# A fused attention and gated-MLP kernel: half-row turns and projections in the first head, two scalings on GpSimd, a half-row filler at the end

## The chip, the cores and the metric

The kernel runs on one core of a Trainium2 chip. The metric is device time in microseconds, the median of several executions. The core has TensorE (PE in the profile; its weight loads are the row PEld), VectorE (DVE), ScalarE (ACT), GpSimd (POOL), and DMA queues issued from several of them (SP issues most). Each engine works through its own list of instructions in order and waits on semaphores that other engines raise.

## The reference, cut to what matters

```python
x = A_x                                   # (1, 2048, 640), bf16
xn = _layernorm(x)                        # per row, eps 1e-5
q = (xn @ wq)                             # 32 heads of 192
p = softmax(q @ k_cache^T * 192 ** -0.5)  # 2048 keys per head
s = (p @ v_cache) @ wo                    # (6144 -> 640)
h = silu(xn @ w1) * (xn @ w3)             # 640 -> 1536
g = silu(h @ w2)                          # 1536 -> 640
return x + s * g
```

All matrices are bf16. The keys and values are inputs; only the queries are projected.

## The kernel before, in words

**Tiles.** The 2048 query rows are 16 tiles of 128 (`ln_*` functions take a tile number) or 4 chunks of 512 (`qb`). The 2048 keys of a head are taken in 8 pairs `p` of 2 x 128. `(qb, p)` below is chunk and pair of a head. The normalised rows are kept transposed in `xnT` (640 columns as 5 blocks `c` of 128 partitions, 2048 rows), and `xnS` is the same with the two 64-partition halves exchanged, copied by DMA (`swap_rows`, L344).

**One pair.** `scores` (L445) does three steps of two matmuls that use 64 rows of the array each (row halves `ROWS`), into a PSUM buffer of the pool `ps_st` (tag `st2`, two buffers). `weights` (L451) is the exponential on ScalarE, with a bias `nb` that bounds the scores so that no running maximum is needed. `values` (L491) multiplies with the values, again on two row halves, into the banks `ob0` and `ob1`; `evict` takes these to SBUF on VectorE at the end of a chunk. `advance` strings this together and leaves three or four groups of value matmuls undone, so that TensorE has work while ScalarE makes the next exponential. It also runs `extra`, work put between a pair's scores and the next pair's.

**The bound `nb`.** It needs the largest absolute query and key entries: `maxima` or a reduction on VectorE, `bound`, and an all-reduce over the partitions on GpSimd (L402). In the first head every chunk has its own `nb` (`next_bound`), later heads have one (`finish_head`). A reduction called `warm` (L539) is put early in the first head.

**The first head.** Rows are normalised while the first head already runs. `ln_stats` (VectorE) or `ln_sum` and `ln_squares` (ScalarE, for the tiles in `ASUM`) give mean and variance, `ln_root` the inverse deviation (ScalarE), `ln_scale` (L251) the scaled row `xn`. Then it is transposed: tiles 0 to 7 on TensorE (`ln_turn`, L259, copied out at L260), tiles 8 to 15 by a transposing DMA from SP's queue (`ln_send`, L271). The first head's projection (`project_chunk`, branch `h == 0`, L318) uses all 128 rows of the array; that of later heads (L323) uses `xnT` and `xnS` on two row halves. Both fill one `st2` buffer with qA (128 columns) and qF; copies give qS (qA with halves exchanged, GpSimd, L329) and qD (half of qF, GpSimd, L333). The third scoring step reads qD and qF.

**Order.** Every instruction given to `pin` keeps the order in which the program text issues it on its engine. The order in the first head is written out by hand: `posts` (after a pair), `extra_at` (inside it), `behind_at` and `key_at` (reductions for the second head). The second head's keys and values are loaded (`load_keys`) after `(1, 3)`, `(1, 5)` and `(1, 6)` of the first.

**The end.** In the last head `hidden_last` (L661) computes one block of hidden units on two row halves, for each chunk, from `xnT` and `xnS`. When the last pair's scores are done, TensorE fills the wait for the last exponentials with `ffn_hidden(0, 1)` (L636, 128 rows). Then the rest of the hidden units, `ffn_out` (L795) and `output_tile` (L774) follow. The weights `w2_sb` (L751) are loaded into memory that `xnS` leaves free.

## Time and profile before

| what | value |
|---|---|
| median of 3 executions | 1941.55 us (1941.48 to 1941.87) |
| the profiled execution | 1941.69 us, its span 1939.8 us |
| TensorE busy | 1931.3 us, VectorE 1097.1, ScalarE 1213.7, GpSimd 464.8 |
| opening, 0 to 16.5 us | TensorE busy 13.70 us |
| chunk 0 of the first head, 16.5 to 29.3 | 12.48 of 12.80 |
| chunk 1, 29.3 to 44.4 | 15.05 of 15.10 |
| chunk 2, 44.4 to 59.5 | 15.04 of 15.10 |
| chunk 3, 59.5 to 75.8 | 16.30 of 16.30 |
| heads 2 to 32, 75.8 to 1634 | 1558.20 of 1558.20 |
| end of the last head, 1634 to 1650 | 15.95 of 16.00 |
| MLP, 1650 to 1726 | 75.82 of 76.00 |
| output, 1726 to 1939.8 | 208.75 of 213.80 |

How to read it: the span runs from the first to the last instruction of the profiled execution. Rows in order of time give start, duration, engine, line, operation, output and inputs, count, and in brackets the idle time of that engine ahead of it with what ended it; rows of the same kind that lie close are merged into one, from the first start to the last modelled end. Matmuls are pipelined and their ends modelled, so distances between starts tell more than durations. Two matmuls on different row halves run at the same time. `POOLq` marks the instructions of GpSimd's sequencer, which don't count as busy.

### The profile page before, as it was taken

To read this page: it belongs to the slowest core of one execution; us is meant where nothing else is said; L and a number is where in the kernel's file an instruction comes from. 1 tells how busy PE (TensorE), PEld (TensorE's weight loads), DVE (VectorE), ACT (ScalarE), POOL (GpSimd) and SP (SyncE) were. 2 spreads that over 40 slices of the span, in tenths; PEclk is the share of its full clock that TensorE was granted. 3 is DMA by queue.
4 is the path that set the end of the run, shared out by engine and by line. 5 is a ranking of instruction groups with operands and counts; after the bars stand their busy time and mean duration, and the time that the engine had idled before them with its cause. 6 is when DMAs were issued, how large, how long until landed. Compare 5 with 4: busy or idle time off the path is not lost.

```text
span 1939.8 us, 60573 instructions
## 1 busy us (share of the span) xinstructions
PE 1931.3 (100%) x27228; PEld 1317.1 (68%) x27237; DVE 1097.1 (57%) x2267; ACT 1213.7 (63%) x1180; POOL 464.8 (24%) x769
## 2 busy tenths in 40 slices
PE   9999999999999999999999999999999999999998
PEld 5666666666666666666666666666666776577776
DVE  8765656565656565666665666656665655521111
ACT  7777777777767677777777777777777777210000
POOL 3432222222222222233222222222222210000000
PEclk9999999999999999999999999999999999999999
DMA  7621212121212222232222222212121103937882
GB/s 173 130 71 42 79 42 79 41 66 40 61 42 64 53 54 63 58 73 68 63 50 71 49 71 50 71 41 79 41 79 41 39 10 116 278 73 135 152 154 55
DMA packets 325098, 146.44 MB, mean 75 GB/s; under 512 B 275984, under 2 KB 317936, under 8 KB 324832
## 3 DMA queue, kind: packets, MB, share of 16 engines
q1 hardware_dynamic: 311184, 110.90, 24.3%
q0 software_dynamic: 8832, 26.55, 5.6%
q10 hardware_dynamic: 4816, 5.05, 1.0%
q8 instruction: 215, 3.52, 0.8%
q14 instruction: 51, 0.42, 0.1%
HBM read 56.23 MB, written 31.98 MB: 45 GB/s over the span
## 4 chain that ended last, share of the span: by engine, by line
PE 99%; ACT 0%; DVE 0%; issue 0%; POOL 0%
PE obank L491 35%; PE st L445 34%; PE ps L323 14%; PE ps_s L774 11%; PE ps_f L795 3%; PE ps_gu L636 1%; PE ps L661 0%; PE ps L318 0%; PE fill L204 0%; ACT xnT L260 0%; ACT pT L451 0%; PE pst L259 0%; POOL qS L329 0%; ACT qA L325 0%; DVE ones_w L166 0%
## 5 line engine op out<-in xcount | busy, mean ns | idle before, releaser
L451 ACT ACTIVATE pT<-st,nb 128x1024 bf16<-128x1024 f32 x1016 | 1130.4, 1113 | 438.7 <-PE st L445 437.3
L491 PEld LDWEIGHTS <-pT 64*128 64x128 bf16 x16384 | 713.2, 94 | 242.3 <-ACT pT L451 0.6
L491 PE MATMUL obank<-vt,pT 64*128 64x193 bf16 x16384 | 851.8, 243 | 0.1
L461 DVE COPY osum<-obank 128x386 f32<-128x386 f32 x256 | 142.3, 556 | 550.1 <-PE obank L491 550.1
L445 PE MATMUL st<-qS,KM 64*128 64x512 bf16 x1024 | 385.1, 376 | 0.5 <-POOL qS L329 0.3
L445 PE MATMUL st<-qA,KM 64*128 64x512 bf16 x1024 | 385.1, 376 | 0.0
L445 PE MATMUL st<-qA,KT 64*128 64x512 bf16 x1024 | 385.0, 376 | 0.0
L445 PE MATMUL st<-qS,KT 64*128 64x512 bf16 x1024 | 385.0, 376 | 0.0
L445 PE MATMUL st<-qF,KT 64*128 64x512 bf16 x1024 | 385.0, 376 | 0.0
L445 PE MATMUL st<-qD,KT 64*128 64x512 bf16 x1024 | 385.0, 376 | 0.0
L329 POOL COPY qS<-qA 64x512 bf16<-64x512 bf16 x256 | 188.7, 737 | 520.9 <-DVE qA L325 495.6
L445 PEld LDWEIGHTS <-KT 64*128 64x128 bf16 x4096 | 201.5, 94 | 135.5 <-issue 0.4
L323 PE MATMUL ps<-xnT,wq 64*128 64x512 bf16 x1240 | 288.1, 376 | 0.0
L323 PE MATMUL ps<-xnS,wq 64*128 64x512 bf16 x1240 | 286.9, 376 | 0.0
L774 PE MATMUL ps_s<-wo_sb,oT 128*128 128x320 bf16 (+2 forms) x1535 | 208.8, 299 | 0.1
L323 PEld LDWEIGHTS <-wq 64*128 64x128 bf16 x2480 | 120.4, 94 | 116.3
L774 PEld LDWEIGHTS <-oT 128*128 128x128 bf16 x1536 | 148.4, 98 | 60.4
L468 DVE TENSOR_TENSOR ostage<-osum,rl_all 128x384 bf16<-128x384 f32 x256 | 153.0, 598 | 9.0 <-DVE rl_all L467 0.3
L462 DVE TENSOR_TENSOR osum<-osum,obank 128x386 f32<-128x386 f32 x256 | 142.6, 557 | 8.9
L348 DVE TENSOR_REDUCE st<-KT 128x1 f32<-128x512 bf16 (+1 forms) x189 | 122.0, 685 | 1.2
L779 DVE SCALAR_TENSOR_TENSOR tmp<-ps_s,g_all 128x320 f32<-128x320 f32 (+2 forms) x32 | 15.6, 487 | 176.0 <-PE ps_s L774 176.0
L445 PEld LDWEIGHTS <-KM 64*128 64x128 bf16 x2048 | 100.5, 94 | 17.5 <-issue 2.3
(112 smaller groups left out, 1139.9 us busy)
## 6 DMA issues: line engine op xcount, KB each, us to landing
o_scr<-ostage SPq DMA_DIRECT2D x64, 384.0 KB, 2.8
vt<-in_A_v_cache_dram SPq DMA_DIRECT2D x62, 384.0 KB, 4.9
wo_sb<-in_A_wo_dram POOLq DMA_DIRECT2D x1, 7680.0 KB, 31.3
wq<-in_A_wq_dram POOLq DMA_DIRECT2D x31, 160.0 KB, 3.1
hT_scr<-hblk SPq DMA_DIRECT2D x16, 256.0 KB, 2.9
xnS<-xnT POOLq DMA_DIRECT2D x8, 320.0 KB, 8.0
xt<-in_A_x_dram POOLq DMA_DIRECT2D x16, 160.0 KB, 9.1
wq<-in_B_w_dram POOLq DMA_DIRECT2D x31, 80.0 KB, 2.6
```

The costliest lines, as they stand in the source:

```text
L323: pin(nc.tensor.matmul(halves[t], lhsT=wq[ROWS[t], s, :], rhs=xs[ROWS[t], s // 2, qs], start=(s == 0), stop=(s == 2 * DC - 1)))
L329: keep(nc.gpsimd.tensor_copy(out=qS[ROWS[t], qs], in_=qA[ROWS[1 - t], qs]))
L348: pin(nc.vector.tensor_reduce(out=heads[h]["st"][:, j, k:k + 1], in_=heads[h]["L"]["KT"][:, j, c0:c1], axis=AX.X, op=ALU.max, apply_absolu ...
L445: pin(nc.tensor.matmul(st2[:, t * 512:(t + 1) * 512], lhsT=k, rhs=q[ROWS[t], qs], start=(s == 0), stop=(s == 2)))
L451: pin(nc.scalar.activation(out=pT2[:], in_=st2[:], func=ACT.Exp, scale=SCALE, bias=nb[:]))
L461: pin(nc.vector.tensor_copy(out=osum[:], in_=ov[:, 0, :, 0:DH + 1]))
L462: pin(nc.vector.tensor_tensor(out=osum[:], in0=osum[:], in1=ov[:, 1, :, 0:DH + 1], op=ALU.add))
L468: pin(nc.vector.tensor_tensor(out=ostage[:, b * 2:b * 2 + 2, hg * DH:(hg + 1) * DH], in0=osum[:, :, 0:DH], in1=rl.unsqueeze(2).to_broadcas ...
L491: pin(nc.tensor.matmul(acc["o"][b][:, r, (j % 2) * 256:(j % 2) * 256 + DH + 1], lhsT=pT2[ROWS[r], t * 512 + j * P:t * 512 + (j + 1) * P], ...
L636: pin(nc.tensor.matmul(ps[:, o:o + 512], lhsT=w_sb[:, c, (fl - 1) * P:fl * P], rhs=xnT[:, c, qs], start=(c == 0), stop=(c == DC - 1)))
L774: pin(nc.tensor.matmul(ps, lhsT=oT[:, k, :], rhs=wo_sb[:, k, c0:c1], start=(k == 0), stop=(k == OC - 1)))
L795: pin(nc.tensor.matmul(ps[:, pi * 512:pi * 512 + c1 - c0], lhsT=lhs[fc], rhs=w2_sb[:, fc, c0:c1], start=(fc == 0), stop=(fc == FC - 1)))
```

## The change: what it does

- `ASUM` loses tile 15: its statistics come from VectorE (`ln_stats`), not from ScalarE.
- `ln_scale` takes an engine; tiles 8 to 11 are scaled on GpSimd, two at a time, after `(0, 5)` and `(0, 7)`. Tiles 12 to 15 stay on VectorE.
- `next_turn` (tiles 4 to 7) transposes each 128-column block as two 64-row halves, each with the identity's half, and both copies are made on VectorE.
- `first_project(0, qb)` for chunks 1 to 3 becomes `half_project(qb, 0)` and `(qb, 1)`, in two successive pairs. Each contracts the two row halves separately into the two halves of an `st2` buffer; ScalarE copies one half to SBUF (`part`), VectorE adds the other.
- The second head's key and value loads come two pairs, and one pair, later.
- `hidden_last` for the last chunk takes the place of `ffn_hidden(0, 1)` in the drain, and `ffn_hidden(0, 1)` goes to the loop behind.

```diff
@@ -177,7 +177,7 @@
             pin(nc.vector.tensor_tensor(out=ident_bf[b, b], in0=cols[b, :], in1=rows[b, :], op=ALU.is_equal))
         nsub = 2
         mv = lnx.tile([P, NQT, nc.vector.BN_AGGR_DIM], F32, name="mv")
-        ASUM = {1: 0, NQT - 1: 1}
+        ASUM = {1: 0}
         sums = lnx.tile([P, len(ASUM)], F32, name="sums")
         sqs = lnx.tile([P, len(ASUM)], F32, name="sqs")
         nmean = lnx.tile([P, len(ASUM)], F32, name="nmean")
@@ -243,12 +243,12 @@
 
         scaled = {}
 
-        def ln_scale(i0):
+        def ln_scale(i0, eng=nc.vector):
             scaled[i0] = []
             for i in range(i0, i0 + 2):
                 xn = xnp.tile([P, D], BF16, tag="xn", name="xn")
                 act = i in ASUM
-                pin(nc.vector.tensor_scalar(out=xn[:], in0=x_all[:, i, :], scalar1=a_col(nmean, i) if act else mv[:, i, 0:1],
+                pin(eng.tensor_scalar(out=xn[:], in0=x_all[:, i, :], scalar1=a_col(nmean, i) if act else mv[:, i, 0:1],
                                             scalar2=rstd[i], op0=ALU.add if act else ALU.subtract, op1=ALU.mult))
                 scaled[i0].append(xn)
 
@@ -262,11 +262,20 @@
                     for t, cp in enumerate(copies)]
 
         def next_turn(i0):
-            for copy in ln_turn(i0, (nc.scalar.copy, nc.vector.tensor_copy)):
-                copy()
-
-        def ln_send(i0):
-            ln_scale(i0)
+            pst = ps_st.tile([P, 2, 1024], BF16, tag="st2", name="pst")
+            for t, xn in enumerate(scaled.pop(i0)):
+                for c in range(DC):
+                    for r in range(2):
+                        c0 = (2 * c + t) * DT
+                        pin(nc.tensor.transpose(out=pst[:, r, c0:c0 + DT], in_=xn[ROWS[r], c * P:(c + 1) * P],
+                                                identity=ident_bf[ROWS[r], ROWS[r]]))
+            for r in range(2):
+                pin(nc.vector.tensor_copy(
+                    out=xnT[:, :, i0 * P:(i0 + 2) * P].rearrange("p c (t r q) -> p c t r q", t=2, r=2)[:, :, :, r, :],
+                    in_=pst[:, r, 0:D].rearrange("p (c t q) -> p c t q", c=DC, t=2)))
+
+        def ln_send(i0, eng=nc.vector):
+            ln_scale(i0, eng)
             for t, xn in enumerate(scaled.pop(i0)):
                 pin(nc.sync.dma_start_transpose(out=xnT[:, :, (i0 + t) * P:(i0 + t + 1) * P], in_=xn[:]))
 
@@ -547,14 +556,32 @@
                 key_shift(h)
 
         def first_project(h, qb):
-            if h == 1 and qb == 0:
-                start_head(1)
-            maxima = project_chunk(h, qb, nc.vector.tensor_copy if h == 0 else nc.scalar.copy)
-            if h == 0:
-                maxima()
+            if qb == 0:
+                start_head(h)
+            behind.append(project_chunk(h, qb, nc.scalar.copy))
+
+        def half_project(qb, t):
+            hd = heads[0]
+            wq, st, qA, qF, qS = hd["L"]["wq"], hd["st"], hd["qA"], hd["qF"], hd["qS"]
+            qs = slice(qb * 512, (qb + 1) * 512)
+            ps = ps_st.tile([P, 1024], F32, tag="st2", name="ps")
+            for c in range(DC):
+                for r in range(2):
+                    pin(nc.tensor.matmul(ps[:, r * 512:(r + 1) * 512], lhsT=wq[ROWS[r], t, c, :], rhs=xnT[ROWS[r], c, qs],
+                                         start=(c == 0), stop=(c == DC - 1)))
+            q, r0 = ((qA, 0), (qF, PGW))[t]
+            part = lnp.tile([P, 512], F32, tag="part", name="part")
+            pin(nc.scalar.copy(out=part[:], in_=ps[:, 0:512]))
+            pin(nc.vector.tensor_tensor(out=q[:, qs], in0=ps[:, 512:1024], in1=part[:], op=ALU.add))
+            if t == 0:
+                for r in range(2):
+                    pin(nc.gpsimd.tensor_copy(out=qS[ROWS[r], qs], in_=qA[ROWS[1 - r], qs]))
+            else:
+                pin(nc.gpsimd.tensor_copy(out=hd["qD"][:, qs], in_=qF[PGW:P, qs]))
+            pin(nc.vector.tensor_reduce(out=st[r0:P, 3 + t, qb:qb + 1], in_=q[r0:P, qs], axis=AX.X, op=ALU.max,
+                                        apply_absolute_value=True))
+            if t == 1:
                 next_bound(qb)
-            else:
-                behind.append(maxima)
 
         def steps(*fs):
             return lambda: [f(*a) for f, *a in fs]
@@ -564,27 +591,32 @@
             (0, 1): ((ln_root, 4), (ln_stats, 6), (ln_scale, 4)),
             (0, 2): ((ln_stats, 7),),
             (0, 3): ((ln_root, 6), (ln_scale, 6), (ln_stats, 8)),
-            (0, 4): ((ln_stats, 9), (ln_stats, 10), (ln_stats, 11)),
-            (0, 5): ((ln_root, 8, 4), (ln_send, 8)),
-            (0, 6): ((ln_send, 10),),
+            (0, 4): ((ln_stats, 9), (ln_stats, 10)),
+            (0, 5): ((ln_root, 8, 2), (ln_send, 8, nc.gpsimd)),
+            (0, 6): ((ln_stats, 11),),
+            (0, 7): ((ln_root, 10, 2), (ln_send, 10, nc.gpsimd)),
             (1, 2): ((ln_stats, 12), (ln_stats, 13), (swap_rows, 1)),
             (1, 3): ((ln_stats, 14), (swap_rows, 2)),
-            (1, 4): ((ln_root, 15, 1), (ln_send, 14)),
+            (1, 4): ((ln_stats, 15),),
+            (1, 5): ((ln_root, 15, 1), (ln_send, 14)),
             (2, 1): ((swap_rows, 3),),
         }
         extra_at = {
             (0, 3): ((next_turn, 4),),
             (0, 4): ((next_turn, 6),),
-            (0, 5): ((first_project, 0, 1),),
+            (0, 5): ((half_project, 1, 0),),
+            (0, 6): ((half_project, 1, 1),),
             (1, 1): ((first_project, 1, 0),),
-            (1, 4): ((ln_root, 12, 3), (ln_sum, 15), (ln_squares, 15), (ln_send, 12), (first_project, 0, 2)),
+            (1, 4): ((ln_root, 12, 3), (ln_send, 12), (half_project, 2, 0)),
+            (1, 5): ((half_project, 2, 1),),
             (2, 1): ((first_project, 1, 1),),
-            (2, 4): ((first_project, 0, 3),),
+            (2, 4): ((half_project, 3, 0),),
+            (2, 5): ((half_project, 3, 1),),
             (3, 1): ((first_project, 1, 2),),
             (3, 4): ((first_project, 1, 3),),
         }
         behind_at = ((2, 2), (2, 6), (3, 3), (3, 6))
-        key_at = ((2, 3), (2, 6), (2, 7), (3, 2), (3, 3), (3, 4))
+        key_at = ((2, 5), (2, 6), (2, 7), (3, 2), (3, 3), (3, 4))
         behind = []
         for qb in range(NQB):
             for p in range(NPAIR):
@@ -594,9 +626,9 @@
                     behind.pop(0)()
                 for f, *a in posts.get((qb, p), ()):
                     f(*a)
-                if (qb, p) == (1, 3):
+                if (qb, p) == (1, 5):
                     heads[1]["L"].update(load_keys(1, hold=True))
-                if (qb, p) in ((1, 3), (1, 5), (1, 6)):
+                if (qb, p) in ((1, 5), (1, 6), (1, 7)):
                     heads[1]["L"]["rest"].pop(0)()
                 if (qb, p) == (2, 6):
                     loads[2] = load_keys(2, hold=True)
@@ -700,7 +732,7 @@
                             gated.append(swiglu_chunk(h // 2, heads[h - 1]["qF"], hd["qF"], c))
                     if h + 1 < H:
                         post.append(project_chunk(h + 1, qb))
-                    else:
+                    elif qb < NQB - 1:
                         post.append(hidden_last(qb))
 
                 for p in range(NPAIR):
@@ -719,7 +751,7 @@
                                 finish_head(h + 1)
                         elif p > 3 and key_slots and (h > 1 or qb > 0):
                             next_keys(h + 1, key_slots)
-                    elif p == 3:
+                    elif p == 3 and post:
                         gated.append(post.pop()())
             heads.pop(h - 1, None)
 
@@ -739,11 +771,11 @@
         load_hT(0)
         while len(parts) > 2:
             parts.pop(0)()
-        rest = ffn_hidden(0, 1, ps_st.tile([P, 1024], F32, tag="st2", name="ps_gu"))
+        gate = hidden_last(NQB - 1)
         load_hT(1)
         while parts:
             parts.pop(0)()
-        rest()
+        gate()()
         late.pop(0)()
     kvstack.close()
 
@@ -807,7 +839,7 @@
         pools = (dsb, otp, ps_st)
         with tc.issue_after(acc["store"].ins):
             tiles = [load_tile(pools, i) for i in range(3)]
-        for fl in range(2, FC - FCP):
+        for fl in range(1, FC - FCP):
             ffn_hidden(0, fl, tail_ps("ps_gu"))()
         for qb in range(NQB):
             if qb + 1 < NQB:
```

## The prediction

> **What bounds the kernel now.** I read the page first, then the first head in order of time (that is where nearly all of the edits are), then the drain behind the last head. The page's busy rows and its chain say that TensorE is the bound from end to end:
>
> ```profile
> span 1939.8 us, 60573 instructions
> PE 1931.3 (100%) x27228; PEld 1317.1 (68%) x27237; DVE 1097.1 (57%) x2267; ACT 1213.7 (63%) x1180; POOL 464.8 (24%) x769
> ...
> PE 99%; ACT 0%; DVE 0%; issue 0%; POOL 0%
> ```
>
> So only two things can move the end: fewer microseconds on TensorE, or a place where TensorE must wait. TensorE in order of time, around a first-head projection on all 128 rows (L318) and one on two 64-row halves (L323):
>
> ```profile
> 37.35 0.57 PE L491 MATMUL obank<-vt,pT 64*128 64x193 bf16 x8
> 37.85 2.33 PE L318 MATMUL ps<-xnT,wq 128*128 128x512 bf16 x9
> 40.11 0.39 PE L445 MATMUL st<-qS,KM 64*128 64x512 bf16 x1
> ...
> 46.36 0.50 PE L491 MATMUL obank<-vt,pT 64*128 64x193 bf16 x8
> 46.70 0.38 PE L323 MATMUL ps<-xnT,wq 64*128 64x512 bf16 x1
> ...
> 48.85 0.38 PE L445 MATMUL st<-qS,KM 64*128 64x512 bf16 x1
> ```
>
> Eight value matmuls take 0.33 us (16 of them advance the chain by 0.67). From 37.68 to 40.11 the full-row projection holds TensorE 2.43 us; from 46.70 to 48.85 the half-row one holds it 2.15. The difference, 0.28 us, is the price of going from half rows to full rows and back. At 23.76 to 26.12 it is 0.21, at 52.80 to 55.22 0.27.
>
> The rows that decide the case are GpSimd's, in order of time and by the two lines that change its code:
>
> ```profile
> L65 POOLq MODIFY_POOL_CONFIG  x2: 11/11/11, 0.8 to 0.9; - x2
> ...
> L539 POOLq MODIFY_POOL_CONFIG  x2: 57/57/57, 17.9 to 18.0; - x2
> ...
> 8.90 0.09 POOL L354 MEMSET sh<- 64x1 f32 x1 [8.44 <-issue]
> ...
> 24.33 0.40 POOL L539 PARTITION_ALL_REDUCE warm<-nbb  x1 [6.63 <-issue]
> 27.46 1.27 POOL L329 COPY qS<-qA 64x512 bf16<-64x512 bf16 x2 [2.73 <-DVE qA L325]
> 28.79 0.61 POOL L333 COPY qD<-qF 64x512 bf16<-64x512 bf16 x1
> 29.79 0.57 POOL L402 PARTITION_ALL_REDUCE nb<-ns  x1 [0.40 <-DVE ns L399]
> ```
>
> GpSimd is told at 18.0 to change its code, and the reduction that needs the new code starts at 24.33: 6.33 us in which nothing else runs there. At the start it is 0.9 to 8.90, 8.0 us. After the warm-up reduction no further change of code occurs in this kernel; the copies in between need none.
>
> **The change, part by part.**
>
> *Scalings on GpSimd.* The instruction lists settle what the diff does not show. In the changed program GpSimd has, after the two qS copies of chunk 1: code change, scaling of tiles 8 and 9, qD copy of chunk 1, code change, the bound's reduction for chunk 1, code change, scaling of tiles 10 and 11, and, after chunk 2's qD copy, code change and the bound for chunk 2. That is four more changes, in a queue that runs in order. L stands for one of them, 6.33 us by the L539 row. Its ends: below, nearly nothing (no row shows a short one); above, the 8.0 of the start.
>
> A scaling of 128x640 on GpSimd is in no row. GpSimd's 64x1024 key copy takes 1.04 us, 1.0 ns per element, so 0.65 us below; twice the copy's rate, 1.3 us, above, for two arithmetic steps. I take 1.0, two for 2.0 us.
>
> Stall 1. On VectorE the work ahead of the first half's sum is, from 20.08 (the last row before it ends at 20.04): two turn copies of 0.49, two scalings 0.80, statistics of tile 8 1.03, two copies 0.98, statistics of tiles 9 and 10 2.06, the sum 0.72 (by the 128x386 addition's 0.557): 26.65. The same queue gave its cast at 26.69 to 27.33 before. GpSimd: qS copies 1.27 to 28.0, L, scalings 2.0, qD 0.61, L, reduction 0.57, with gaps: the bound of chunk 1 is there at 31.3 + 2L = 43.95. The exponential that needs it (`(1,0)`) began at 30.39 before. So stall 1 is 0.9 + 2L, 13.55 us; TensorE stops in `(1,0)`, first at its third scoring step for qD (37 us), then ahead of the second head's first projection, whose buffer that exponential holds: 31.58 becomes 45.1.
>
> Stall 2. From there to chunk 2's projection is 6.2 us of TensorE work, so it is wanted at 51.3. Its tiles 10 and 11 are scaled from 43.95 + L = 50.3 to 52.3, and the transposing DMA lands 3.4 us later (median of xnT<-xn in the first head; 2.6 to 9.8): 55.7. Stall 2 is 4.4 us, or L - 1.9.
>
> Stall 3. Counted from chunk 2's first half: half 1.08, scores 0.65, values 0.67; the second half needs the buffer that the first half's addition frees at 2.64, so it runs 2.70 to 3.78; scalar copy to 4.58, addition to 5.32, qD to 6.0, L, reduction: the bound at 12.9. Scores of `(2,0)` end at 7.4, their exponential would start at 7.6, and 0.3 us of slack lies ahead of the next use of its buffer. Stall 3 is L - 1.3 = 5.05. Chunk 3 pays no change of code: its bound is there at 6.8, wanted at 7.6.
>
> Sum of the three: 4L - 2.3 = 23.0 us. Nothing absorbs it: the stretch from 75.8 to 1634 us has TensorE busy throughout.
>
> The Trainium skill, page "GPSIMD Engine Reference", section "Instruction dispatch", has about 6 us (5.95 measured) for the first call to freshly loaded code, with no instruction of its own in a profile; with that figure the same sum would be 21.5. The L539 row (6.33) bears it out, and speaks against this change.
>
> *Restart of TensorE.* The opening shows TensorE slow after idleness: the first 15 fills (128x512) take 5.66 us; at the later pace of L318 (ten of that size from 37.85 to 40.11) they would take 3.4, so 2.3 us are lost. Waits of up to 1.5 us (11.8 to 13.3) lose nothing visible. For a wait of some 5 us the ends are 0 and 2.3; it is far above the harmless one, so I take 2.3 for stall 3. Behind stall 1 it costs nothing more, since stall 2's end is set by GpSimd and the DMA, and only shrinks to about 2 us, near the harmless kind.
>
> The Trainium skill, page "TensorE: Matmul & The Clock Gate", Part 1 on the clock gate, lets the clock fall to half after an idle window of about 3.4 us and takes as much busy time to restore it; by that rule, an estimate from its figures, stall 3 would cost 1.7 more instead of 2.3. The granted clock reads 1.00 throughout this trace, so only the opening's pace bears on it.
>
> *Half-row projections.* Chunks 2 and 3 would save 0.28 and 0.27 by the lines above, but each half takes a score buffer of its own, and the second waits 0.3 us for VectorE's addition (2.40 to 2.70 above). From the start of the projection to the next chunk's scores it was 6.64 and 6.71; I get 6.75: a loss of 0.15 in all, not a gain. The six scalar copies of 0.59 fit between exponentials.
>
> *Half-row turns.* Ten transposes with both switches held TensorE 0.9 us; twenty half ones lie between 0.55 and 0.85 by the pace of the value pairs. The first turn ends on a wait for the exponential (0.21 at 20.19), and both end long before stall 1, so 0. Tile 15's statistics move from ScalarE to VectorE (1.03 us), off the path; 0.
>
> *End filler.* In the drain the full-row filler held TensorE from 46.86 to 49.22 (in 1600s) and the half-row one takes 2.16: 0.2 saved. Ten pairs move later, ten full-row matmuls move behind them, no change otherwise. But the weights `w2` (named w_sb in the page) reuse xnS, which the filler now reads:
>
> ```profile
> 1638.76 1.06 POOL L751 DMA_DIRECT2D w_sb<-in_B_w_dram  x1 [46.56 <-PE ps L661]
> ...
> 1660.79 2.34 PE L795 MATMUL ps_f<-w_sb,hT 128*128 128x320 bf16 x16
> ```
>
> Issue goes to 1647.3 on this clock; with its 9.1 us it lands at 1656.4, 4.2 us before the first use at 1660.6. Ends: 0, and some 3 us if it took as long as the slowest hT load (12.2) and more. I take 0. The wait on GpSimd's queue holds three small loads behind it; the 31.3 us load of wo waits for the last store anyway and is wanted at 1726.
>
> *Second keys* are issued two pairs later, with some 20 us to their first use against 12.6 us for the slowest key load; 0.
>
> Sum: 23.0 + 2.3 + 0.15 - 0.2 = +25.25. The profiled execution took 1941.69 (span 1939.8 and 1.9 around it), 0.14 over the median 1941.55: **1966.9 us**.
>
> **Rivals.**
> 1. *The code change costs little when the code was there before* (other side). GpSimd's chain alone then gives stall 1 = 0.9, the rest nothing: +0.9 + 0.15 - 0.2, 1942.5, no change. It decides at L below 1.5 (0.9 + 2L + 0.2 = 4.1). For it: both rows are first loads. Against it: a first load is all the trace has, and both are over 6 us. 0.06.
> 2. *In between*, L of 2 to 4.5: 1949 to 1958. For it: DMA was busy in both rows, here it is nearly idle at 28 us. 0.08.
> 3. *The scaling's code takes the 8.0 us of its own row*: stalls 1 and 2 grow by 1.67 each, 1970.3. Against it: the start of the program may be in that row. 0.17.
> 4. *w2 comes late*, on top of the likeliest: 1968 to 1970; the margin of 4.2 us speaks against it. 0.04.
> 5. *The half rows' gain alone*, with no stall, would be 0.28 + 0.27 + 0.21 + 0.2, about 1 us: no rival for "faster" by itself.
>
> **How the numbers follow.** The likeliest, L near 6.3, has 0.65: 1966.9. Its own range is 1960 to 1973: scalings of 0.65 to 1.3 us (-1.4 to +1.2), landing 2.6 (-0.8), restarts of 0 to two (-2.3 to +2.3), L down to 5.6 (-3). The range reaches 1958 to 1977: rival 3 and rival 4 inside it, L of 8 on all four changes at the top, rival 1 and most of rival 2 left out. About 0.2% (3.9 us) is what a measurement of this kernel can tell from no change. Rival 1's 0.06 is split, 0.02 faster and 0.04 same; the rest, 0.94, is slower.
>
> **What would show it.** GpSimd: four more changes of code, each with some 6 us of idleness behind it, and scalings of about 1 us. TensorE: idle ahead of st<-qD for GpSimd's qD, ahead of the second head's first projection, of chunk 2's first half for xnT, and in chunk 2. ScalarE: two waits for nb. The stretch between the second head and the drain unchanged. Wrong if these waits are under 2 us, or if TensorE's waits are for other things.

## The result, and the profile after

The changed kernel takes 1976.7 us (1974.97 to 1977.11, five runs) against 1941.55 us before: a ratio of 1.0178, 95% interval 1.0167 to 1.019, so 35 us slower. The forecast was 1966.9 us in a range of 1958 to 1977: the sign and the mechanism held, the size was 10 us short, and the time lies 0.3 us inside the upper end of the range, outside the likeliest case's own 1960 to 1973. The profiled execution took 1976.19 us, its span 1974.1, 34.3 more than the span before.

The page's span, busy rows and chain (by engine) of the changed kernel:

```profile
span 1974.1 us, 60700 instructions
PE 1939.4 (98%) x27287; PEld 1322.9 (67%) x27287; DVE 1095.3 (55%) x2268; ACT 1215.1 (62%) x1181; POOL 475.0 (24%) x773
...
PE 97%; DVE 1%; ACT 1%; POOL 1%; issue 0%; DMA 0%; POOLq 0%
```

TensorE is 8.1 us busier with the same arithmetic, and idle for about 26 us more. GpSimd is busy for 10 us more, which is the four scalings (tiles 8 to 11; the title counts them as two, since they are posted in two pairs). The next lines show first the instructions that change GpSimd's code (for each line the number of records, two for a change, their ns, and the start of the first and the last), then GpSimd in order of time (start, duration, and in brackets the idle time ahead).

```profile
L251 POOLq MODIFY_POOL_CONFIG  x4: 4/44/83, 27.8 to 47.1; - x4
L251 POOL TENSOR_SCALAR xn<-x_all,mv,rstd x4: 2488/2503/2517, 34.9 to 56.5; 128x640 bf16<-128x640 bf16 x4
...
L411 POOLq MODIFY_POOL_CONFIG  x4: 8/8/8, 40.8 to 70.4; - x4
```

```profile
26.48 1.27 POOL L578 COPY qS<-qA 64x512 bf16<-64x512 bf16 x2 [2.36 <-DVE qA L575]
34.93 5.01 POOL L251 TENSOR_SCALAR xn<-x_all,mv,rstd 128x640 bf16<-128x640 bf16 x2 [7.17 <-issue]
40.00 0.61 POOL L580 COPY qD<-qF 64x512 bf16<-64x512 bf16 x1
46.67 0.40 POOL L411 PARTITION_ALL_REDUCE nb<-ns  x1 [6.06 <-DVE rl_all L476]
53.99 5.01 POOL L251 TENSOR_SCALAR xn<-x_all,mv,rstd 128x640 bf16<-128x640 bf16 x2 [6.92 <-ACT qF L335]
...
76.08 0.48 POOL L411 PARTITION_ALL_REDUCE nb<-ns  x1 [5.88 <-DVE rl_all L476]
```

There are four changes of code. The start of the code-changing record (27.8, 40.8, 47.1 and 70.4) to the instruction that needs the new code is 7.1, 5.9, 6.9 and 5.7 us. The releasers named in the brackets had long been done; it is the new code that GpSimd waits for. A scaling of 128x640 takes 2.5 us. It is not other engines that slow it: from 34.93 to 39.94 TensorE, VectorE and ScalarE are all idle, and two scalings take 5.01 us, as they do from 53.99 to 59.00, when TensorE and ScalarE work.

What TensorE waited for in the whole execution (us in total, times, longest), and its rows at the three long waits:

```profile
PE st L454 <- POOL qD L580: 10.9, 1, 10.9
PE ps L332 <- ACT pT L460: 8.5, 2, 4.3
PE ps L570 <- DMA xnT<-xn: 4.4, 1, 4.4
PE obank L500 <- DVE osum L471: 1.8, 2, 1.3
```

```profile
40.66 0.58 PE L454 MATMUL st<-qD,KT 64*128 64x512 bf16 x1 [10.93 <-POOL qD L580]
48.27 0.58 PE L332 MATMUL ps<-xnT,wq 64*128 64x512 bf16 x1 [4.16 <-ACT pT L460]
61.73 2.32 PE L570 MATMUL ps<-xnT,wq 64*128 64x512 bf16 x10 [4.43 <-DMA xnT<-xn]
77.76 0.58 PE L332 MATMUL ps<-xnT,wq 64*128 64x512 bf16 x1 [4.32 <-ACT pT L460]
```

The two waits for ScalarE's `pT` are waits for the bound: ScalarE's own answer is

```profile
ACT pT L460 <- POOL nb L411: 20.4, 2, 15.4
```

The second part of the loss is the pace behind the waits. A half-row matmul of 64x512 took 0.38 us in the first head before; at 40.66, 48.27 and 77.76 it takes 0.58 and more. Busy time by stretch, with the granted clock of TensorE as the column behind POOL's (the rows from 60 and from 76 us begin within a wait, in which the clock still reads 1.00 up to 60.64 and 77.71; in the work behind it reads 0.50):

```profile
24.00:30.00 6.00, 5.65 (x76) 3.54 (x73) 4.42 (x11) 4.09 (x7) 1.33 (x3) 1.00 0.02 4
48.20:52.50 4.30, 4.23 (x21) 2.33 (x22) 1.17 (x4) 1.02 (x2) 0.00 (x0) 0.50 0.02 4
60.00:64.00 4.00, 2.27 (x12) 1.04 (x14) 0.00 (x0) 0.00 (x0) 3.75 (x6) 0.58 0.83 154
68.00:72.00 4.00, 4.00 (x70) 3.02 (x68) 2.42 (x6) 3.10 (x5) 0.61 (x1) 1.00 0.54 102
76.00:80.00 4.00, 2.24 (x12) 0.96 (x13) 1.57 (x3) 2.12 (x2) 0.48 (x1) 0.71 0.98 188
```

TensorE's landmarks in the two profiled executions give the ledger. Each row is the distance from the landmark above it, after less before.

| stretch on TensorE | before | after | more |
|---|---|---|---|
| start to the second head's first projection | 31.58 | 48.27 | 16.69 |
| to chunk 2's first projection (before: the 37.76 at which it could have started on half rows) | 6.18 | 13.46 | 7.28 |
| to the first scores of chunk 2, `(2, 0)` | 6.64 | 9.24 | 2.60 |
| to the second head's second projection | 2.30 | 6.79 | 4.49 |
| to `(2, 2)` | 2.15 | 3.80 | 1.65 |
| an eviction in the first head's last chunk, PE waits at 98.1 | | | 0.49 |
| the last head's last chunk, PE waits at 1671.35 | | | 1.31 |
| the drain behind it | | | -0.2 |
| sum | | | 34.3 |

The row 16.69 holds 0.21 that the opening took longer, which differs from execution to execution (-0.03 to 0.69 in the runs below). The agreement with the spans to a tenth is partly luck: the table leaves out a drift between the two executions, 33.36 us at the second head's last projection (101.27 us), 32.83 near 1173 us and 33.00 near 1618, and the waits for evictions cost 0.67 and 1.49 by the neighbouring starts where the rows say 0.49 and 1.31.

### The profile page after: what moved, and what is told of

It is laid out like the page before. It is cut to its first block, busy times and chain, and to the rows that moved or that the text cites. A ratio compares the mean times of both kernels' runs of the same rounds, so it can differ in the third digit from the quotient of the medians.

```text
span 1974.1 us, 60700 instructions
## 1 busy us (share of the span) xinstructions
PE 1939.4 (98%) x27287; PEld 1322.9 (67%) x27287; DVE 1095.3 (55%) x2268; ACT 1215.1 (62%) x1181; POOL 475.0 (24%) x773
## 3 DMA queue, kind: packets, MB, share of 16 engines
q10 hardware_dynamic: 4816, 5.05, 1.0%
## 4 chain that ended last, share of the span: by engine, by line
PE 97%; DVE 1%; ACT 1%; POOL 1%; issue 0%; DMA 0%; POOLq 0%
PE obank L500 34%; PE st L454 33%; PE ps L332 14%; PE ps_s L806 11%; PE ps_f L827 3%; PE ps_gu L668 1%; POOL xn L251 1%; PE ps L693 0%; PE ps L570 0%; ACT pT L460 0%; DVE osum L471 0%; DVE osum L470 0%; DMA x_all<-in_A_x_dram 0%; DVE st L210 0%; DMA xnT<-xn 0%
## 5 line engine op out<-in xcount | busy, mean ns | idle before, releaser
L454 PEld LDWEIGHTS <-KT 64*128 64x128 bf16 x4096 | 202.7, 94 | 147.4 <-issue 12.8
```

The source lines that it names most:

```text
L454: pin(nc.tensor.matmul(st2[:, t * 512:(t + 1) * 512], lhsT=k, rhs=q[ROWS[t], qs], start=(s == 0), stop=(s == 2)))
```

## The experiments

G stands for the theory that the scalings on GpSimd make the time: four changes of code and four slow scalings in a queue on which the bound waits, and a TensorE that is slow after each wait. Its rivals are named with each run. The times of a group are compared with runs of the kernel before on the same chip (1941.84, 1941.94, 1941.76 and 1941.83 us in the four groups, 1941.55 beside the changed kernel), so differences between groups are uncertain by some 0.4 us.

### The scalings back on VectorE, then the other parts one by one

First run: the changed kernel with only the engine of the four scalings undone.

```diff
-            (0, 5): ((ln_root, 8, 2), (ln_send, 8, nc.gpsimd)),
+            (0, 5): ((ln_root, 8, 2), (ln_send, 8)),
...
-            (0, 7): ((ln_root, 10, 2), (ln_send, 10, nc.gpsimd)),
+            (0, 7): ((ln_root, 10, 2), (ln_send, 10)),
```

> The changed kernel with its four GpSimd scalings back on VectorE, all else as changed. Theory G (code changes and slow scalings in GpSimd's queue hold qD, the bound and xnT, and TensorE restarts slowly after each wait): 32.7 of the 35 us go, and the half rows' small gains in chunks 0 and 1 (0.4 us) show, so about 1943. Rival H (the half-row sums, which pass through ScalarE, VectorE and a PSUM buffer twice, are what holds TensorE): most of the loss stays, 1955 or more.

Measured: 1945.19 us, ratio 1.0017 (1.0008 to 1.0026). Of 35.1 us, 31.8 are the scalings' engine (35.1 - 3.35, each against its own runs of before). Rival H, 1955 or more, is out. The remaining 3.35 us is 2 us more than G had, and its parts come out by undoing further. On top of this run, the end as before:

```diff
-                    elif qb < NQB - 1:
+                    else:
...
-        gate = hidden_last(NQB - 1)
+        rest = ffn_hidden(0, 1, ps_st.tile([P, 1024], F32, tag="st2", name="ps_gu"))
```

> As the run before, and the end as it was before the change (full-row filler, the last chunk's hidden block in its second pair). If the last head's 1.31 us wait for an eviction comes from the block taken out of that chunk, 1.1 us go: about 1941.9. If that wait has another cause, the old filler costs its 0.2 us: about 1943.2.

Measured: 1943.8 us, 1.4 less where 1.1 less was expected if the block taken out is the cause, and the 1.31 us wait is gone from the trace; the 2 us by which the run before missed are still in the time. And on top of that, the second head's keys at their old places:

```diff
-        key_at = ((2, 5), (2, 6), (2, 7), (3, 2), (3, 3), (3, 4))
+        key_at = ((2, 3), (2, 6), (2, 7), (3, 2), (3, 3), (3, 4))
...
-                if (qb, p) == (1, 5):
+                if (qb, p) == (1, 3):
...
-                if (qb, p) in ((1, 5), (1, 6), (1, 7)):
+                if (qb, p) in ((1, 3), (1, 5), (1, 6)):
```

> As the run before, with the second head's key loads and key reductions at their old places. If the 0.49 us wait for an eviction at the start of chunk 3 comes from a key reduction that was moved behind the half-row sums on VectorE, it shrinks: about 1941.4, at or a little under the kernel before. If it comes from the sums themselves: no change, 1941.9.

Measured: 1943.27 us, 0.53 less, and the wait for an eviction in the first head (0.6 us in the run before it) is gone. Loads and key reductions were put back together, so this run does not tell the two apart. The mirror image of the second step is the kernel before with the new end and nothing else:

```diff
-                    else:
+                    elif qb < NQB - 1:
...
-        rest = ffn_hidden(0, 1, ps_st.tile([P, 1024], F32, tag="st2", name="ps_gu"))
+        gate = hidden_last(NQB - 1)
```

> The kernel before with the new end alone. By the prediction's term: 0.2 us less, 1941.35. By the trace of the changed kernel: 0.2 less for the filler and 1.31 more for the eviction, 1942.65.

Measured: 1943.17 us, ratio 1.0007 (0.9998 to 1.0016), 1.33 more than before where the trace had let expect 1.11; its eleven runs (1942.79 to 1943.85) lie above all of before's (1941.53 to 1942.56). TensorE's row at the place:

```profile
1639.32 1.01 PE L491 MATMUL obank<-vt,pT 64*128 64x193 bf16 x20 [1.31 <-DVE osum L462]
```

Taking `hidden_last` out of the last chunk's pair 1 removes its 2.16 us of matmuls (1636.14 to 1638.30 before) from between the previous chunk's last values and the first values of this one; TensorE then comes to the value banks before VectorE has emptied them, and stands for 1.31 us. The work removed was cover. So the ledger of the small parts is: new end 1.4, later keys 0.5, and 1.4 for what else changed in the first head, which is the half rows and the statistics and roots that were moved with them.

### A code change without a scaling

The kernel before, with one scaling of a single column on GpSimd ahead of chunk 1's bound:

```diff
+            if qb == 1:
+                tiny = stt.tile([P, 1], BF16, tag="tiny", name="tiny")
+                pin(nc.gpsimd.tensor_scalar(out=tiny[:], in0=x_all[:, 4, 0:1], scalar1=mv[:, 4, 0:1], scalar2=rstd[4],
+                                            op0=ALU.subtract, op1=ALU.mult))
             hd["nb"].append(bound(hd["km"][:], hd["st"][:, 3:5, qb]))
```

> The kernel before with one scaling of a single column (128x1) on GpSimd ahead of chunk 1's bound, its result read by nobody: two code changes on the way of the first bound and next to no scaling. Theory G (each code change holds GpSimd 5.7 to 7.1 us, as the four in the profile of the changed kernel did, and TensorE then starts again at a granted clock near half): the bound of chunk 1 lands 12 to 13 us late, the second head's first projection starts about 12.3 us later than the 31.58 us of before, and its matmuls take 1.7 to 3.9 us more, so 1955.7 to 1957.9 us. Theory S (it is the length of the scalings, 2.5 us each, and what stands behind them, that stops the kernel, and the code change is a by-product of the long instruction): about 1942 us.

Measured: 1958.13 us, ratio 1.0082 (1.0065 to 1.0098), 16.2 us more, just above G's 1957.9; the rival's 1942 is out. GpSimd in order of time, and the one long wait on TensorE:

```profile
37.17 0.40 POOL L409 TENSOR_SCALAR tiny<-x_all,mv,rstd 128x1 bf16<-128x1 bf16 x1 [7.21 <-issue]
44.19 0.40 POOL L402 PARTITION_ALL_REDUCE nb<-ns  x1 [6.62 <-issue]
```

```profile
45.80 0.58 PE L323 MATMUL ps<-xnT,wq 64*128 64x512 bf16 x1 [13.48 <-ACT pT L455]
```

0.4 us of arithmetic whose result nobody reads costs 16 us: 7.21 of idleness ahead of it, 6.62 behind it, 13.48 of waiting on TensorE. The span is 16.8 longer; the projection starts 14.22 later than before (0.55 of it from a longer opening in this execution), so 2.6 us come behind the wait. The stretch in which that projection runs shows why:

```profile
45.50:50.00 4.50, 4.21 (x20) 2.37 (x21) 0.00 (x0) 1.25 (x2) 0.00 (x0) 0.50 0.00 0
```

### Other work of the same size on GpSimd

The changed kernel with plain copies in place of the scalings, same tiles, same places; it leaves out the normalisation of tiles 8 to 11:

```diff
+                if eng is nc.gpsimd:
+                    pin(eng.tensor_copy(out=xn[:], in_=x_all[:, i, :]))
+                    scaled[i0].append(xn)
+                    continue
```

> The changed kernel with its four scalings on GpSimd replaced by four plain copies of the same 128x640 tiles on GpSimd, at the same places and with the same readers; the normalisation of tiles 8 to 11 is left out. Theory G (the code change belongs to the scaling as a kind of instruction, the rest of its cost to its own 2.5 us): no code change ahead of the copies nor ahead of the bounds behind them, copies of 0.7 us each by the 64x512 copies' 0.61 us, so the last product of chunk 1 waits about 1.4 us and the time is that of the changed kernel with its scalings on VectorE (1945.2 us) plus 0 to 2.5 us: 1945 to 1948 us. Theory B (any 128x640 work placed there on GpSimd holds up the copies and bounds behind it): 1970 us or more.

Measured: 1945.17 us, ratio 1.0016 (1.0007 to 1.0025), the same as with the scalings on VectorE (1945.19). GpSimd around the copies:

```profile
28.19 1.38 POOL L252 COPY xn<-x_all 128x640 bf16<-128x640 bf16 x2
29.63 0.61 POOL L584 COPY qD<-qF 64x512 bf16<-64x512 bf16 x1
30.66 0.38 POOL L415 PARTITION_ALL_REDUCE nb<-ns  x1 [0.42 <-DVE ns L412]
30.91 1.44 POOL L252 COPY xn<-x_all 128x640 bf16<-128x640 bf16 x2
```

No code change, 0.7 us for a tile, and the place in the queue costs next to nothing (TensorE waits 0.2 us for qD). So it is neither the place nor the tile's size: it is that a change of code stands ahead of this kind of instruction and ahead of the reduction behind it, and that it takes 2.5 us where a copy takes 0.7.

### Two code changes or four, and behind the bound

The changed kernel with its four scalings posted together:

```diff
-            (0, 4): ((ln_stats, 9), (ln_stats, 10)),
-            (0, 5): ((ln_root, 8, 2), (ln_send, 8, nc.gpsimd)),
-            (0, 6): ((ln_stats, 11),),
-            (0, 7): ((ln_root, 10, 2), (ln_send, 10, nc.gpsimd)),
+            (0, 4): ((ln_stats, 9), (ln_stats, 10), (ln_stats, 11)),
+            (0, 5): ((ln_root, 8, 4), (ln_send, 8, nc.gpsimd), (ln_send, 10, nc.gpsimd)),
```

> The changed kernel with its four scalings posted together behind pair 5 of the first head's chunk 0: two code changes instead of four, but all 10 us of the scalings ahead of chunk 1's bound. Theory G (each code change costs 5.7 to 7.1 us on the path, each scaling 2.5): the bound lands near 53 us, so the second head's first projection starts about 22 us later than before's 31.58 us, TensorE starts again at 2 to 3 us more, chunk 2's transposed rows wait for nothing further, and the 1.8 us of the end and the evictions stay: about 1968 us. Theory S (the length of the scalings alone): the same 10 us of scalings, so no less than 1976 us.

Measured: 1968.21 us, ratio 1.0136 (1.0119 to 1.0153), 8.5 us less than the changed kernel (8.9 if each is taken against its own runs of before) with the same scalings on the same engine. The wait for qD grows to 15.48 us, the second head's first projection starts at 53.56, 21.98 later than before (22 was expected), and the waits for chunk 2's transposes and for chunk 2's bound are gone. Theory S, no less than 1976 us, is out.

The kernel before with its scalings on GpSimd at their old places in the program, which is behind chunk 1's bound:

```diff
-            (0, 5): ((ln_root, 8, 4), (ln_send, 8)),
-            (0, 6): ((ln_send, 10),),
+            (0, 5): ((ln_root, 8, 4), (ln_send, 8, nc.gpsimd)),
+            (0, 6): ((ln_send, 10, nc.gpsimd),),
```

> The kernel before with its four later scalings on GpSimd in their old places of the program, which is behind chunk 1's bound: the code changes there and back are off the way of the first bound, and the scalings' 10 us are too. Theory G: the second head's first projection starts at about 31.6 us as before; the code change ends near 38 us, the four scalings near 48 us, and the transposed rows of tiles 8 to 11 land near 50.3 us, where chunk 2's projection wants them at 37.8 us: 12.5 us of waiting, 3 to 4 us of TensorE at half its clock, and about 2 us of chunk 2's bound behind the change back: about 1960 us. Theory V (what costs is only that the scalings stand ahead of chunk 1's bound; behind it they are covered): about 1942 us.

Measured: 1961.84 us, ratio 1.0103 (1.0086 to 1.012). TensorE's two waits:

```profile
50.86 4.42 PE L318 MATMUL ps<-xnT,wq 128*128 128x512 bf16 x10 [12.61 <-DMA xnT<-xn]
65.67 0.37 PE L323 MATMUL ps<-xnT,wq 64*128 64x512 bf16 x1 [3.50 <-ACT pT L451]
```

The wait for the transposes is 12.61 us (12.5 expected), the one for chunk 2's bound 3.50 (2 expected). A full-row projection that took 2.33 us before takes 4.42 here. Behind the shorter wait the granted clock still reads 1.00 at first (the matmul at 65.67 takes 0.37 us), and 0.50 from 65.92 to 69.34. The rival, that only the place ahead of chunk 1's bound costs, falls: behind it the same work stands ahead of the transposes that chunk 2 wants.

### TensorE kept busy through the waits

The changed kernel, with the first scoring step repeated twenty times ahead of two pairs of the first head:

```diff
-            for s, step in enumerate(steps):
+            for n, step in enumerate((steps[0],) * again + steps):
+                s = max(0, n - again)
...
+            again = 20 if hd["h"] == 0 and (qb, p) in ((1, 4), (2, 1)) else 0
```

> The changed kernel with the first scoring step issued twenty times more in the first head's pairs 4 of chunk 1 and 1 of chunk 2, into the same bank and started anew each time, so the result stays the same and TensorE has some 8 us of work where it stood idle ahead of chunk 2's first half and in chunk 2. Theory G (after the idle time TensorE runs at a granted clock of 0.50 to 0.58, which costs 2.60 us behind the first half and 1.65 us behind the third stall, beside the waits themselves): both go, 4.25 us less, while the added matmuls outlast the waits by 0 to 2 us: 1972.5 to 1974.5 us, with a granted clock of 1.00 from 61 us on. Theory N (those two stretches are long because of the waits for GpSimd's results, whatever the clock): no less than 1976.7 us.

Measured: 1971.68 us, ratio 1.0153 (1.0136 to 1.017), 5.0 us less than the changed kernel with 80 matmuls more, and 0.8 below G's range. The same stretches of time as above, of this kernel (the second head's second projection begins at 74.72 here; from 69 to 75 us the clock reads 1.00 as well):

```profile
60.00:64.00 4.00, 3.40 (x46) 2.05 (x43) 1.73 (x4) 3.01 (x5) 3.51 (x6) 1.00 0.66 139
...
76.00:80.00 4.00, 4.00 (x64) 2.91 (x62) 1.85 (x4) 2.64 (x4) 1.73 (x3) 1.00 1.07 257
```

From chunk 2's first projection to `(2, 0)` it is 6.69 us (9.24 in the changed kernel), and from the second head's second projection to `(2, 2)` 2.16 (3.80): 2.55 and 1.64 us are back, 4.2 together as expected. The spans of the two profiled executions differ by 4.5; the rest of it is that this one came to chunk 2 0.6 us earlier (61.14 instead of 61.73; the idle times ahead of its first scaling and its first bound were 6.91 and 5.80 instead of 7.17 and 6.06), and small differences the other way. The theory that these stretches are long because of the waits alone falls: the time that GpSimd's results take is still there (`(2, 0)` to the second projection is 6.89 us against 6.79), only filled with work that is thrown away.

### The half rows in the first head

With scalings, end and keys put back, 1.4 us remained. Three runs went after it. The first has the turns alone on the kernel before:

```diff
-            for copy in ln_turn(i0, (nc.scalar.copy, nc.vector.tensor_copy)):
-                copy()
+            pst = ps_st.tile([P, 2, 1024], BF16, tag="st2", name="pst")
...
+                    for r in range(2):
+                        c0 = (2 * c + t) * DT
+                        pin(nc.tensor.transpose(out=pst[:, r, c0:c0 + DT], in_=xn[ROWS[r], c * P:(c + 1) * P],
```

> The kernel before with the later turns on row halves and nothing else of the change. Theory G (the turns are worth the 0.2 us that they gained in the changed kernel's first head, and both copies fit on VectorE): 1941.5 to 1942 us, no difference that can be measured. Theory T (the half rows' 1.4 us that remained with the scalings, the end and the keys put back comes from the turns): 1943.2 us.

Measured: 1943.5 us, 1941.82 to 1945.61 over eleven runs, ratio 1.0007 (0.9998 to 1.0016). That is 1.7 more than before at the median, with a spread of 3.8 us where the kernel before has about 1.0, which neither theory had. T's 1943.2 is near the median, but not for T's reason: in the kernel whose 1.4 us it was to explain (scalings, end and keys put back), TensorE waits for no transpose. In the profiled run, the slowest of the eleven, the projections of chunk 2 and chunk 3 wait for the transposing DMA:

```profile
39.67 2.32 PE L327 MATMUL ps<-xnT,wq 128*128 128x512 bf16 x10 [1.89 <-DMA xnT<-xn]
...
56.94 1.24 PE L327 MATMUL ps<-xnT,wq 128*128 128x512 bf16 x5 [1.77 <-DMA xnT<-xn]
```

The turns themselves gain: counted from `(0, 0)`, `(1, 0)` comes 0.41 us earlier (13.62 to 29.20, against 13.30 to 29.29). In the profile of before the transposes had come in time. That both copies now stand on VectorE is not the cause: it scales tiles 8 to 11 at 29.39 here and at 29.53 before. What grew is the time from issue to landing, with a median of 5.5 us and up to 12.8 where before had 3.4 and up to 9.8. On SP's queue the second head's keys, a transposing DMA too, go out between the two sets of `xn` transposes, so the next run issues them later:

```diff
-                if (qb, p) == (1, 3):
+                if (qb, p) == (1, 5):
...
-                if (qb, p) in ((1, 3), (1, 5), (1, 6)):
+                if (qb, p) in ((1, 5), (1, 6), (1, 7)):
```

> The kernel before with the turns on row halves and the second head's keys at their new places, behind the transposes of the first head's last rows; nothing else of the change. Theory G (the turns gain 0.46 us in chunk 0, and the 1.9 and 1.8 us for which TensorE waited for transposes when the turns were changed alone come from the second keys' own transposing DMA, which shared the queue with them; they go when the keys are issued later): 1941.3 to 1942.3 us, with a narrow spread again; up to 0.5 us of it a wait for an eviction in chunk 3, as where the keys were late before. Theory N (the transposes are late because of the turns, or for the DMAs' own spread): 1943.5 us with the waits still there.

Measured: 1941.82 us, 1941.13 to 1942.61, ratio 0.9999 (0.999 to 1.0008). The median is back and the spread down to 1.5, as G had it. But a wait of 0.67 for the transposes of chunk 2 is left in its profile, with no key load yet issued; so the keys are not all of chunk 2's wait. Each profile is of one execution, the slowest of its eleven; that the later keys take away chunk 3's wait and narrow the spread fits both runs, and how a late key load and the turns act together on the landings is not shown. It is the best version measured with any of the change in it, and no better than the kernel before.

Last, the kernel with scalings, end and keys put back, and two pieces of work moved out of the half sums' way (against that kernel):

```diff
-            (0, 4): ((ln_stats, 9), (ln_stats, 10)),
-            (0, 5): ((ln_root, 8, 2), (ln_send, 8)),
-            (0, 6): ((ln_stats, 11),),
-            (0, 7): ((ln_root, 10, 2), (ln_send, 10)),
+            (0, 4): ((ln_stats, 9), (ln_stats, 10), (ln_stats, 11)),
+            (0, 5): ((ln_root, 8, 4), (ln_send, 8)),
+            (0, 7): ((ln_send, 10),),
...
-            (1, 5): ((ln_root, 15, 1), (ln_send, 14)),
+            (1, 5): ((ln_root, 15, 1), (ln_send, 12), (ln_send, 14)),
...
-            (1, 4): ((ln_root, 12, 3), (ln_send, 12), (half_project, 2, 0)),
+            (1, 4): ((ln_root, 12, 3), (half_project, 2, 0)),
```

> The changed kernel with scalings on VectorE, the old end and the old key places (1943.3 us), and two things put elsewhere: the statistics of tile 11 back to pair 4 and one square root for tiles 8 to 11, so that ScalarE no longer waits for them ahead of chunk 1's first exponentials, and the scalings of tiles 12 and 13 behind chunk 2's half sums. Theory G (the rest of 1.4 us is those two waits, 1.3 us in chunk 1 and 0.5 us in chunk 2): 1941.3 to 1942 us, as before or a shade under. Theory T (it is the half sums themselves, which need an eviction by ScalarE and an addition by VectorE ahead of each bound): 1943 us or more.

Measured: 1942.97 us, ratio 1.0006 (0.9997 to 1.0015), only 0.3 less: G is out, and T, the half sums themselves, is what is left. Chunk 2 gave back its part: from the second head's first projection to its second it is 15.25 us (15.61 with the work in the way, 15.12 before). Chunk 1 did not: with the statistics of tile 11 ahead of it, VectorE's addition for the first half comes later, and the second half waits 0.81 us for it; the wait ahead of the second head's projection shrinks from 0.99 to 0.28, and that projection starts no earlier (32.99, against 32.86). So my theory held for chunk 2 and not for chunk 1. VectorE was busy for 13.68 of the 15 us from 16 to 31 before the change, and the half sum adds an addition of 0.7 us ahead of the bound; in both orders tried, what was put ahead of it showed up again. That no order would do better is not shown.

## Why the prediction came out as it did

**What bounds the kernel.** Right: between the second head and the last one the distance to before stays within 0.5 us, and TensorE is busy throughout.

**The code change, L = 6.33.** Right. The four were 7.1, 5.9, 6.9 and 5.7 us, 25.6 together against 25.3. The single-column scaling showed that a change of code costs this with next to no work behind it, the copies that it takes this kind of instruction, and the four scalings in one go that the number of changes counts. Rivals 1 and 2 (a change that is cheap once the code has been there) are excluded: each of the two sets had to come back in full. Rival 3, 8.0 us, is out too, though its direction was right, since to the scaling's code it is 6.7 to 7.6 us in the five kernels with such changes (7.6 once, with the scalings behind the bound) and back to the reduction's 5.7 to 6.4, each from the start of the code-changing record. The Trainium skill, page "GPSIMD Engine Reference", section "Instruction dispatch", has about 6 us (5.95 measured) for the first call to freshly loaded code; these runs agree in kind and lie at 5.7 to 7.6.

**The scaling, 1.0 us (0.65 to 1.3).** Wrong, and this is the term that failed most: 2.5 us, outside both ends. I bounded it by GpSimd's copies and allowed two arithmetic steps to double them. The copies of the same tile take 0.7 us, so the arithmetic costs 3.6 times the copy. Stall 1 holds two of them (+3.0 us), and so does stall 2 (+3.0).

**Stall 1, 13.55.** Measured 16.48 (16.69 less the opening's 0.21): +2.93, the scalings. The places were right: first qD, then ahead of the second head's first projection.

**Stall 2, 4.4.** Measured 7.28: +2.88; scalings +3.0, code change +0.6, and a landing of 2.57 instead of 3.4.

**Stall 3, 5.05.** Measured 4.49: the code change behind it was 5.7.

**Restart of TensorE, 2.3, once.** The size was near, the count was not. The size was taken from the opening, where the granted clock reads 1.00, so that it came near is partly luck. The harmless wait of 1.5 us was misread too: the rows from 11.79 to 13.30 hold matmuls up to 13.03 and a wait of 0.27, and the longest wait behind the opening's first is 0.71. I took stall 2's wait to shrink to about 2 us, "near the harmless kind"; with the scalings' real length it was 4.43, and TensorE came out of it at half clock: 2.60 us there and 1.65 behind stall 3, 4.25 against 2.3. Filling both waits with matmuls gave 4.2 of that back, with a granted clock of 1.00. The rule of the Trainium skill, page "TensorE: Matmul & The Clock Gate", Part 1 (half the clock after an idle window of about 3.4 us), which put a restart at an estimated 1.7, agrees with these runs: waits of 3.50 us and more were followed by a granted clock of 0.50, waits up to 1.89 us by 1.00, and no wait lay between, so the threshold itself is not measured here. The cost was 1.65 to 2.6.

**Half-row projections, +0.15, and turns, 0.** Small, and wrong in chunk 1, which I costed at nothing beyond what stood in stall 1: without the stalls what is left of the change in the first head costs 1.4 us, and since the turns by themselves gain about 0.4, the half sums and what moved with them cost about 1.8, a difference and not a measurement. Rival 5's gain of about 1 us from half rows showed in no run; the best, turns and keys alone, is level with before. In the changed kernel this is hidden, since the bound waits for GpSimd anyway.

**End filler, -0.2.** The drain did gain 0.2, and `w2` came in time. What failed is "no change otherwise": the block removed from the last chunk had covered an eviction, and 1.31 us of waiting was added in its place.

**Second keys, 0.** Wrong by 0.5: I looked at the load's time and not at the key reductions on VectorE that move with it. With them later, the eviction begins 0.58 us later on VectorE (64.22 against 63.64 with the keys put back).

The differences add up. Measured less predicted: 2.93 + 2.88 - 0.56 (stalls), 1.95 (restarts), 1.31 (eviction at the end), 0.49 (eviction behind the keys), 0.21 (opening), less the 0.15 not separately visible, is 9.06, and 25.25 + 9.06 = 34.3, the difference of the spans. That the time still fell inside the range is luck: its upper end stood for code changes of 8 us, which alone would have given 1973.6, and it was filled by scalings, a second restart and an eviction instead.

## What to carry to other kernels

On GpSimd, look at what the neighbours in its queue are before counting an instruction's own time: here a scaling between two all-reduces cost 12.6 to 13.8 us of code changes, and a copy in the same slot none. Price an operation from a row of the same kind on the same engine; a copy's row bounds arithmetic from below only, so where no row exists the upper end has to be far. When work is taken out of the bounding engine's list, ask what it covered: the next buffer that it reaches earlier may not be free, and a long wait on TensorE (3.50 us and more in these runs) is paid a second time in clock.

## What the runs showed of the hardware that I had not expected

- GpSimd's scaling of 128x640 bf16 takes 2.49 to 2.52 us, also with the other engines idle; its copy of the same tile takes 0.7, and VectorE's scaling 0.44.
- The price of a change of code differs with its direction: 6.7 to 7.6 us to the scaling's, 5.7 to 6.4 to the reduction's, seven of each in five kernels.
- TensorE's granted clock stayed at one half for some time after work had begun again. Read in half-microsecond stretches, the clock of the changed kernel is 1.00 or 0.50, a value between being a stretch that holds a change. It falls at 33.34, 46.99, 60.64 and 77.71 us and rises at 43.58, 53.82, 67.47 and 81.12. Work began again at 40.66, 48.27, 61.73 and 77.76, so half clock lasted 2.9, 5.6, 5.7 and 3.4 us more. With TensorE kept busy, and with the scalings in one go, 3.8 us of work behind the first wait did not end it before the next wait came.
- The distances between these eight changes are 10.24, 3.41, 6.83, 6.82, 6.83, 10.24 and 3.41 us, whole multiples of 3.41, and so are the distances in the other kernels that have any (13.65, 10.24 and 3.42 with the scalings behind the bound; 13.65, 20.48 and 23.89 in three more). In these runs the clock changes only at ticks 3.41 us apart, and it would follow that the cost of a restart depends on where between two ticks the work begins.
- A small change of order can show as spread rather than as a shift: with the turns alone, eleven runs lay from 1941.82 to 1945.61, and with the second keys issued later as well, from 1941.13 to 1942.61.
